# Scoring the last 64 keys of two quads of heads in one group of eight 32x64 tiles, with an issue order written out as a list

## The chip, the core and the metric

One core of a Trainium2 chip runs the whole program. The metric is device time in microseconds (us), the median of several executions. An operation runs on one of four computing engines: TensorE (PE in the profile, its weight loads PEld), VectorE (DVE), ScalarE (ACT) and GpSimd (POOL). SyncE (SP) issues most DMA transfers. Each engine works through its own instructions strictly in the order in which they were issued, and waits at an instruction whose inputs are not there.

## The reference

Four batches of 12 heads, 448 positions, head size 64; then a two-layer perceptron over 1792 tokens of 768 numbers with 2048 hidden units, all in float32.

```python
scores = scale * np.matmul(q, k.transpose(0, 1, 3, 2))
scores = cap * np.tanh(scores / cap)
scores = scores - np.max(scores, axis=-1, keepdims=True)
attn = np.exp(scores)
attn = attn / (np.sum(attn, axis=-1, keepdims=True) + 1e-09)
attn_out = np.matmul(attn, v)
x = attn_out.transpose(0, 2, 1, 3).reshape(B * S, H * D)
h = x @ w_in
out = np.maximum(0.01 * h, h) @ w_out
```

## The kernel before

**Attention.** The 48 heads go in 12 quads of four heads, a quad being two pairs. The head size of 64 is cut in two halves of 32 (`x`), so that a head's keys and queries fill one strip of 32 partitions and the four heads of a quad lie in the four strips of TensorE's array. `scores` (L490 to L506) makes the scores in four groups of keys. Groups 0 to 2 have 128 keys each: four tiles of 32x128 of the array work at once, one for each head, and two passes (`x` 0 and 1) are added (L505). Group `MID` has the last 64 keys: four tiles of 32x64 (L502), each of which uses one half of the columns, so that half the array stands still. Every float32 matmul of the program becomes two in the trace, so one group of scores is 16 matmuls and 16 weight loads. The scores land in the PSUM tiles `sc`, one for each pair, of two banks. ScalarE then takes tanh out of PSUM (L560) and exp in place (L563) into a ring of SBUF tiles `pf` (`exps` in the trace; some more of them lie in `w` for the first half of the pairs). `values` (L550) multiplies them with the value rows in two tiles of 128x64, `middle` (L525) does that for the last 64 keys in four tiles of 64x64. In parallel VectorE or GpSimd add the exponentials up into `t` (L568, L569, L571); from the fourth quad on VectorE transposes and reduces this sum (L592, L593), a matmul with a folding matrix (L597) adds across partitions, and VectorE takes reciprocals (L602), spreads them (L618) and scales the product out of the PSUM tile `po` (L633). `po` has two banks for these pairs, so the product of pair i+2 waits for the scaling of pair i.

**Perceptron.** The first 256 tokens go through both layers in plain float32 (L749, shapes 128x256) while attention still runs, which also brings the weights in: each of the 34 weight blocks is loaded (L657), converted by ScalarE (L686, L692) and VectorE (L694, L697) and stored to scratch memory. The next 512 tokens go through in split form (a rounded part and a rest, three matmuls instead of one; L749, 128x512). The last 1024 tokens go through a seven-product scheme (L1002, L1172). Finished rows of the second layer are transposed into the staging ring `ot` (L793) and stored (L714).

**Order.** Every piece of work is described by `plan.add(rank, cost, fn, ...)`: the engines that it may run on with a cost on each, what it reads and writes. `Plan.issue` (L115) then issues the 2237 steps one by one, taking the one that its cost table says can start first, ties going to the lower rank; ranks come from the formulas plus the tables of offsets in `T`. The engine of a step that may run on several is chosen there too.

**Start.** `cap`, then the keys, then the values of the first quad are issued on the SP queue, the queries on ScalarE's; VectorE computes the scale factors, then turns queries and keys (L481, L483, L484), then the first group of scores starts.

Of the kernel before, what the change touches and what calls it, by code (L numbers as in the profile page):

```python
# [20 lines left out]
    pf=6,  # L21
# [4 lines left out]
    ot=2,  # L26
# [23 lines left out]
    jc=19,  # L50
    ps=245,
# [3 lines left out]
    role={'duo C': -747.31, 'duo U': -735.34, 'duo a': 179.43, 'duo b': 124.52, 'duo d': 590.63, 'duo g': -972.64, 'duo vh': 66.56, 'duo vl': -126.79, 'duo vs': -257.1, 'duo ws dma': -667.59, 'duo z': 232.65, 'last uh': 813.04, 'last ul': -850.97, 'last wq dma': -1627.0, 'pair first first': -711.17, 'pair first.0 zero': -379.79, 'pair first.1 zero': -662.52, 'pair kT': 46.8, 'pair kT first': -31.97, 'pair kT.0 zero': 524.69, 'pair kraw dma': -251.58, 'pair kraw dma first': 172.22, 'pair kraw.0 dma zero': 256.19, 'pair late': -153.04, 'pair pf': 1229.42, 'pair pf exp': -636.67, 'pair pf first': -424.63, 'pair pf first exp': -1045.36, 'pair pf zero exp': -677.25, 'pair pf.0 zero': 476.57, 'pair pf.1 zero': -402.02, 'pair pf.2 zero': -57.0, 'pair pf.3 zero': -163.21, 'pair pf.4 zero': -330.08, 'pair pf.5 zero': -652.4, 'pair pf.6 zero': 135.96, 'pair pf.7 zero': -352.12, 'pair po': 46.47, 'pair po first': 98.34, 'pair po.0 zero': -814.17, 'pair po.1 zero': -331.16, 'pair po.2 zero': 507.3, 'pair po.3 zero': 960.61, 'pair qT': 507.24, 'pair qT first': 646.87, 'pair qT.0 zero': -560.63, 'pair qraw dma': 975.57, 'pair qraw dma first': -463.96, 'pair qraw.0 zero': -220.82, 'pair rs': 101.18, 'pair rt': 291.72, 'pair rt first': -532.24, 'pair rt.0 zero': 685.14, 'pair rt.1 zero': 177.61, 'pair sc': -78.62, 'pair sc first': 29.1, 'pair sc.0 zero': 29.75, 'pair sc.1 zero': -75.32, 'pair sc.2 zero': -234.87, 'pair sc.3 zero': -16.59, 'pair sums': 335.88, 'pair sums first': -694.63, 'pair sums.0 zero': -27.21, 'pair sums.1 zero': 548.07, 'pair sums.2 zero': -823.01, 'pair sums.3 zero': 66.32, 'pair t': -6.69, 'pair t first': -125.0, 'pair t.0 zero': -64.91, 'pair t.1 zero': -171.68, 'pair tT': 87.9, 'pair tail': -78.4, 'pair tot': -77.55, 'pair vc dma': 327.77, 'pair vc dma first': -73.96, 'pair vc.0 dma zero': -782.5, 'pair vc.1 dma zero': 431.37, 'pair wait': -253.82, 'pair x': -397.07, 'pair x first': 799.88, 'pair x.0 zero': 561.7, 'pair x.1 zero': 1748.4, 'pair x.2 zero': 215.71, 'pair x.3 zero': 900.12, 'pair xh': 233.42, 'pair xh first': 393.76, 'pair xh.0 zero': 535.24, 'pair xh.1 zero': 153.8, 'pair xl': -827.07, 'pair xl first': -666.27, 'pair xl.0 zero': 38.95, 'pair xl.1 zero': 1133.45, 'run Bh': 396.97, 'run Bl': -350.58, 'run g': -708.72, 'run late': -69.63, 'run late_T': -85.85, 'run wait_T': -395.49, 'side T': 692.46, 'side sH': -962.56, 'side sL': 132.33, 'sum p dma': -375.81, 'sum pr dma': 163.76, 'sum pre': 201.62, 'tile p': -171.41, 'tile store dma': 143.89, 'tile y': 420.39, 'tile yz': 34.48, 'unit g': -165.47, 'unit gh': 572.6, 'unit gl': -1821.34, 'unit gr first': 303.24, 'unit m': -295.94, 'unit m first': -98.85, 'unit ot': 570.96, 'unit ot first': 459.51, 'unit raw first': -22.51, 'unit scratch dma first': -952.64, 'unit store dma': 697.81, 'unit store dma first': 8.06, 'unit whi': -26.24, 'unit wlo': -50.07, 'unit wr dma first': 296.0, 'unit ws dma': -139.31, 'unit ws first': -9.13, 'x cap dma': -1133.33, 'x fixed_vx': -703.14, 'x fold': 302.79, 'x inv': -323.73, 'x regs': -707.36},  # L55
    pair=[-751.47, -917.18, -160.61, 298.32, 45.73, -549.43, -291.06, 148.77, -108.48, -102.5, 15.65, 416.32, 208.41, 216.63, -339.77, -85.19, -629.45, 975.97, 348.69, 982.9, -64.89, 260.92, -1123.87, -876.4, 0.0, 0.0, 0.0, 0.0, 0.0, 0.0],
# [5 lines left out]
    sum=[-74.38, 94.11, -560.41, -1031.6, 404.68, 85.84, -89.45, -386.3, -39.95, -117.43, -150.24, 303.72, 184.5, 188.74, 749.08, -126.77, -158.74, -502.96, -81.48, -387.42, -616.58, 21.56, 173.92, 18.59],  # L62
    tile=[-209.93, -102.29, -202.36, -40.16, 33.34, -362.19, 26.13, 30.99, -31.31, -32.81, -33.42, -34.86, -439.45, -32.85, 84.22, -60.17, 123.96, 119.05, -402.42, -104.85, -700.26, -6.29, 386.27, 346.62, 581.06, 33.84, 551.59, 123.05],
    phases=[(1000000000.0, {'pe': 33.33, 'dve': 0.44, 'pool': 0.03})],
)


def hundredths(x):
    return round(100 * x)


class Plan:
# [6 lines left out]

    SWITCH = 9
    LAT = {"act": 13, "dve": 12, "pool": 10, "pe": 20}

    def __init__(self):
# [1280 lines left out]
```

## Time and profile before

| | us |
|---|---|
| median of 3 runs | 643.89 (643.75 to 644.42) |
| the profiled execution | 643.21 |
| its span, first to last instruction | 641.4 |
| TensorE busy | 626.4 |
| VectorE busy | 505.3 |
| ScalarE busy | 348.2 |
| GpSimd busy | 149.6 |

The page gives for each engine the time in which it had an instruction in work. Because matmuls overlap each other, a group of matmuls is better read from the chain of work, where each piece counts only the time until the next one took over.

### The profile page before, as it was taken

What the parts mean: (1) busy time and instruction counts of PE and PEld (TensorE: products, weight loads), DVE (VectorE), ACT (ScalarE), POOL (GpSimd) and SP (SyncE); (2) the same over time, 40 slices, a digit from 0 to 9 for tenths busy, and PEclk for the clock granted to TensorE, in tenths of its full rate; (3) what the DMA queues carried; (4) which work ended last, traced back from release to release, by engine and by line L of the source; (5) the groups of instructions that cost most, each with busy time, mean ns of one, the idle gap of its engine ahead of it and who ended that gap; (6) DMA issues with size and microseconds to landing.
All of it is one profiled execution on the core that took longest, in us unless ns stands there. A gap on an engine that the chain in (4) does not pass through costs nothing.

```text
span 641.4 us, 9583 instructions
## 1 busy us (share of the span) xinstructions
PE 626.4 (98%) x3364; PEld 455.4 (71%) x3364; DVE 505.3 (79%) x801; ACT 348.2 (54%) x532; POOL 149.6 (23%) x180
## 2 busy tenths in 40 slices
PE   7999999999999999999999999999999999999996
PEld 4333655565656658686846688888888789999996
DVE  3989899999999987667858896776878999956640
ACT  4998688886856755246436343322334535743311
POOL 1032202311010314765644130130122320002210
PEclk9999999999999999999999999999999999999999
DMA  7974469758849767677774244220112063323422
GB/s 258 366 243 134 160 217 285 235 200 281 250 135 315 254 167 241 201 225 213 200 214 128 66 114 106 66 74 26 61 63 65 26 198 98 99 86 109 135 51 54
DMA packets 106151, 102.95 MB, mean 160 GB/s; under 512 B 29552, under 2 KB 86896, under 8 KB 106096
## 3 DMA queue, kind: packets, MB, share of 16 engines
q1 hardware_dynamic: 105184, 101.02, 52.1%
q10 hardware_dynamic: 912, 1.25, 0.7%
q8 instruction: 28, 0.46, 0.3%
q14 instruction: 27, 0.22, 0.1%
HBM read 77.86 MB, written 24.38 MB: 159 GB/s over the span
## 4 chain that ended last, share of the span: by engine, by line
PE 91%; DVE 5%; DMA 2%; ACT 1%; issue 1%; SPq 0%; DVEq 0%
PE m L749 35%; PE sc L1002 10%; PE po L550 9%; PE sc L1172 8%; PE sc L505 8%; PE po L1172 5%; PE m L1172 5%; PE po L1002 4%; PE sc L502 3%; PE m L1002 2%; PE po L525 1%; DMA raws<-in_k_dram 1%; DVE w L284 1%; DMA cap_sb<-in_cap_dram 1%; PE po L597 1%
## 5 line engine op out<-in xcount | busy, mean ns | idle before, releaser
L749 PE MATMUL m<-bank,ws 128*128 128x256 f32 x384 | 91.8, 388 | 0.0
L749 PEld LDWEIGHTS m<-bank,ws 128*128 128x128 f32 x384 | 70.1, 190 | 25.7 <-issue 10.1
L560 ACT ACTIVATE exps<-sc 128x896 f32<-128x896 f32 (+1 forms) x72 | 58.6, 837 | 49.5 <-PE sc L505 25.5
L277 ACT CAST w<-ws 128x384 fp32r<-128x384 f32 (+3 forms) x83 | 51.3, 632 | 51.2 <-PE m L749 24.5
L505 PE MATMUL sc<-heads 32*128 32x448 f32 x576 | 65.7, 560 | 4.3 <-ACT exps L560 2.0
L284 DVE TENSOR_TENSOR w<-ws,w 128x384 fp32r<-128x384 f32 (+3 forms) x84 | 63.5, 769 | 7.4 <-ACT w L277 5.9
L749 PE MATMUL m<-bank,w 128*128 128x512 f32 x288 | 68.8, 394 | 0.0
L749 PEld LDWEIGHTS m<-bank,w 128*128 128x128 f32 x288 | 53.2, 188 | 16.1 <-issue 4.8
L866 POOL TENSOR_TENSOR raws<-raws 128x128 f32<-128x128 f32 x96 | 55.2, 591 | 31.4 <-DMA raws<-scratch 28.3
L563 ACT ACTIVATE exps<-exps 128x896 f32<-128x896 f32 (+1 forms) x72 | 61.2, 872 | 0.7
L749 PE MATMUL m<-xh,w 128*128 128x512 f32 x192 | 61.2, 394 | 0.1
L505 PEld LDWEIGHTS sc<-heads 32*128 32x128 f32 x576 | 27.0, 184 | 33.8 <-issue 15.1
L550 PE MATMUL po<-exps,norm 128*64 128x448 f32 x232 | 48.8, 549 | 0.0
L749 PEld LDWEIGHTS m<-xh,w 128*128 128x128 f32 x192 | 36.0, 188 | 11.3 <-issue 2.7
L749 PE MATMUL m<-xl,w 128*128 128x512 f32 x96 | 37.4, 389 | 0.0
L284 POOL TENSOR_TENSOR w<-ws,w 128x384 fp32r<-128x384 f32 (+2 forms) x16 | 21.2, 1324 | 62.2 <-ACT w L277 53.7
L550 PEld LDWEIGHTS po<-exps,norm 128*64 128x64 f32 x232 | 14.7, 136 | 28.2 <-issue 21.1
L692 ACT ACTIVATE ws<-bank 128x768 f32<-128x768 f32 (+1 forms) x34 | 29.8, 881 | 8.7 <-PE m L749 8.5
L694 DVE SCALAR_TENSOR_TENSOR bank<-bank 128x768 int32<-128x768 int32 (+1 forms) x34 | 33.0, 977 | 1.8 <-ACT ws L692 1.6
L697 DVE SCALAR_TENSOR_TENSOR ws<-ws,bank 128x768 int32<-128x768 int32 (+1 forms) x34 | 30.5, 900 | 0.4
L686 ACT ACTIVATE bank<-bank 128x768 int32<-128x768 uint8 (+1 forms) x27 | 23.6, 876 | 3.5 <-DMA bank<-in_moe_w_out_dram 1.9
L571 POOL TENSOR_TENSOR norm<-norm,w 64x448 f32<-64x448 f32 x8 | 10.0, 1248 | 62.1 <-DVE norm L569 27.3
(220 smaller groups left out, 1230.8 us busy)
## 6 DMA issues: line engine op xcount, KB each, us to landing
ws<-scratch SPq DMA_DIRECT2D x38, 384.0 KB, 3.4
bank<-in_moe_w_in_dram SPq DMA_DIRECT2D x16, 768.0 KB, 7.4
scratch<-ws SPq DMA_DIRECT2D x22, 384.0 KB, 3.8
raws<-scratch SPq DMA_DIRECT2D x48, 128.0 KB, 3.3
sums<-raws SPq DMA_DIRECT2D x24, 256.0 KB, 3.0
raws<-in_k_dram SPq DMA_DIRECT2D x12, 448.0 KB, 5.6
raws<-in_q_dram SPq DMA_DIRECT2D x11, 448.0 KB, 4.6
norm<-in_v_dram SPq DMA_DIRECT2D x48, 96.0 KB, 3.3
```

What stands on the lines that cost most here:

```text
L277: nc.scalar.copy(o, i)
L284: ENG[eng].tensor_tensor(out=o, in0=a, in1=f32(b), op=ALU.subtract)
L505: nc.tensor.matmul(sc[r // 2][:, r % 2, 0:S], keys(a)[part4[r], x, P * g:P * g + P], queries(c)[part4[r], x], **flags)
L550: nc.tensor.matmul(at("po", 2 * i)[half[j], 0:S], at("vc", i)[:, j, g], pf(g)[:, j if wide(g) == 2 else 0], start=(g == 0), stop=(g == NG ...
L560: a = plan.add(r, {"act": ct}, lambda e, sc=sc, g=g: nc.scalar.activation(pf(g), sc(), AF.Tanh, scale=scale_of["tanh"]), vers("sc", [g]) + ...
L563: plan.add(r + 2, {"act": ct + 0.03}, lambda e, g=g: nc.scalar.activation(pf(g), pf(g), AF.Exp, scale=scale_of["exp"]), (), vers("pf", [g] ...
L694: a = plan.add(rank, {"dve": cv}, lambda e: nc.vector.scalar_tensor_tensor(out=word(1), in0=word(1), scalar=-0x80000000, in1=word(0), op0= ...
L697: plan.add(rank, {"dve": cv}, lambda e: nc.vector.scalar_tensor_tensor(out=z(), in0=z(), scalar=3, in1=word(1), op0=ALU.logical_shift_left ...
L749: nc.tensor.matmul(ps(), l, r, start=begins and some[0] == 0 and i == 0, stop=ends and some[-1] == len(cs) - 1 and i == len(ops) - 1)
L866: return plan.add(rank, cost, lambda e: ENG[e].tensor_tensor(out=o(), in0=a(), in1=b(), op=op), reads, writes, after=after, freed=freed, p ...
L1002: nc.tensor.matmul(ps(), l, r, start=start and x == 0, stop=x == len(ops) - 1, skip_group_check=not start)
L1172: nc.tensor.matmul(ps[t](), l, r, start=start and n0 == 0 and x == 0, stop=n0 == NK - 2 and x == len(ops) - 1, skip_group_check=not start)
```

## The change

- For the first four quads nothing changes in the scores. From the fifth on (`jm=4`) two neighbouring quads, (4,5), (6,7), (8,9) and (10,11), share one group `MID`: quad q's four tiles of 32x64 write bank 0 of the two `sc` tiles, quad q+1's four write bank 1, and `flipped` is turned round for the second quad, so that the eight tiles cover every strip and both column halves. The group is 32 matmuls and 32 weight loads. Its tanh and exp are then 128x896 for each `sc` tile, once for two quads. The second quad's keys and queries must be turned before the first quad's last group (`lead`, `jl=6`).
- The `pf` ring in SBUF grows from 6 to 7 tiles; two of them are kept for the joint group, five are left for the groups 0 to 2 (the tiles in `w` still come on top for the first half). `ot` shrinks from two tiles to one.
- For the first quad the keys are loaded in three transfers, the first 128 keys first and ahead of `cap`; the queries come in two halves; a tanh on one column is put behind them on ScalarE's queue; the turning is cut into four pieces, the first keys and the first half of the queries first, and the scale factors are computed after them.
- `issue` no longer plans: it goes through `STEPS`, a list of all 2237 steps. A number is a step's place in the order of the `plan.add` calls, the letter its engine (p TensorE, a ScalarE, v VectorE, g GpSimd, s SyncE). All offsets in `T` are zero and unused.

```diff
-    pf=6,
+    pf=7,
-    ot=2,
+    ot=1,
+    jm=4,
+    jl=6,
...
+STEPS = """
+    3s 6a 5s 7v 8v 9v 10v 11p 1g 4v 0g 665s 676s 15s 667a 666a 677v 68s 67s 687s 33s 71v 668v 669v 688v 69v 70v 654s 698s 2a 34a 16a 35a 17a 12p
...
-    def issue(self, phases):
+    def issue(self, order):
...
+        issued = set()
+        for item in order.split():
+            n, eng = int(item[:-1]), self.ENGINES[item[-1]]
+            s = steps[n]
...
+            assert deps <= issued and n not in issued and eng in s["cost"], n
+            issued.add(n)
             s["fn"](eng)
...
+    JM = T["jm"]
+    joint = lambda q_: 0 if q_ < JM else 1 + (q_ - JM) % 2
+    mid_of = lambda i: (4 * (i - 2) + 3, 1) if joint(i // 2) == 2 else (4 * i + 3, 0)
...
+            free_ = list(range(n_pf - 2)) + (list(range(n_pf, n_pf + n_more)) if wide_ else [])
+            for g in range(4):
+                for i in (2 * q_, 2 * q_ + 1):
+                    if g == 3:
+                        out[4 * i + g] = -1 if joint(q_) == 2 else n_pf - 2 + i % 2
+                    else:
+                        out[4 * i + g] = free_[turn_ % len(free_)]
+                        turn_ += 1
...
+    def first_loads(n):
+        t, src = raw4("kraw"), rows_of(k)
+        by_tile = lambda a: a[:, 0:4 * MID].rearrange("p (r g) d -> p r g d", g=MID)
+        if n == 0:
+            nc.sync.dma_start(out=by_tile(t)[:, :, 0], in_=by_tile(src)[:, :, 0])
+            nc.sync.dma_start(out=cap_sb, in_=cap.to_broadcast([P, 1]))
+            return
+        nc.sync.dma_start(out=by_tile(t)[:, :, 1:], in_=by_tile(src)[:, :, 1:])
+        nc.sync.dma_start(out=t[:, 4 * MID:], in_=src[:, 4 * MID:])
+
+    def first_queries():
+        t, src = raw4("qraw"), rows_of(q)
+        for h in range(2):
+            nc.scalar.dma_start(out=t[:, HB * h:HB * h + HB], in_=src[:, HB * h:HB * h + HB])
+        nc.scalar.activation(warm, zeros, AF.Tanh)
...
-    flipped = lambda i: i % 2
+    flipped = lambda i: i % 2 ^ (joint(i // 2) == 2)
...
+            for x in range(2):
+                flags = dict(start=x == 0, stop=x == 1)
+                for r in range(4):
+                    if g < MID:
+                        nc.tensor.matmul(sc[r // 2][:, r % 2, 0:S], at("kT", q_)[part4[r], x, P * g:P * g + P], at("qT", q_)[part4[r], x], **flags)
+                        continue
+                    for c in range(2 if joint(q_) else 1):
+                        c_ = half[r % 2 ^ flipped(i0 + 2 * c + r // 2)]
+                        nc.tensor.matmul(sc[r // 2][c_, c, 0:S], at("kT", q_ + c)[part4[r], x, far:S], at("qT", q_ + c)[part4[r], x], **flags)
...
-        plan.issue(T["phases"])
+        plan.issue(STEPS)
```

## Rows read from the trace of the kernel before

**Rows 1.** Page: busy time, granted clock in 40 slices, chain by engine.

```profile
PE 626.4 (98%) x3364; PEld 455.4 (71%) x3364; DVE 505.3 (79%) x801; ACT 348.2 (54%) x532; POOL 149.6 (23%) x180
...
PEclk9999999999999999999999999999999999999999
...
PE 91%; DVE 5%; DMA 2%; ACT 1%; issue 1%; SPq 0%; DVEq 0%
```

**Rows 2.** Busy time of each engine by stage, us from the span's start.

```profile
core 0: us, PE busy (x) PEld busy (x) DVE busy (x) ACT busy (x) POOL busy (x), PEclk, DMA share, GB/s
0.00:36.00 36.00, 30.90 (x182) 13.82 (x184) 24.69 (x46) 27.16 (x36) 5.11 (x17) 1.00 0.93 315
36.00:66.00 30.00, 29.17 (x199) 11.08 (x193) 26.71 (x52) 25.32 (x37) 9.00 (x9) 1.00 0.54 170
...
101.00:231.00 130.00, 130.00 (x776) 76.09 (x775) 123.37 (x194) 98.14 (x133) 19.84 (x14) 1.00 0.75 238
231.00:400.00 169.00, 168.85 (x831) 121.27 (x831) 126.47 (x180) 77.92 (x117) 73.27 (x109) 1.00 0.62 173
...
510.00:642.00 132.00, 122.50 (x694) 120.09 (x692) 87.89 (x141) 51.46 (x96) 14.87 (x9) 0.99 0.35 101
```

**Rows 3.** Chain of work in order of time: start us, us, what.

```profile
75.42 5.38 PE m L749 x24
80.80 1.72 PE sc L505 x16
82.52 2.41 PE po L550 x12
84.92 0.91 PE po L525 x8
...
96.26 1.66 PE sc L502 x16
...
355.03 1.66 PE sc L502 x16
```

**Rows 4.** Weight loads of L502: durations ns min/median/max, and eight at 176.87 us.

```profile
L502 PEld LDWEIGHTS sc<-heads x192: 127/131/132, 18.7 to 355.8; 32*64 32x64 f32 x192
...
176.87 0.21 PEld L502 LDWEIGHTS sc<-heads 32*64 32x64 f32 x8 [0.33 <-issue]
```

**Rows 5.** ScalarE's tanh, shapes apart: busy us, mean ns, idle before.

```profile
L560 ACT ACTIVATE exps<-sc 128x896 f32<-128x896 f32 x56 | 50.5, 919 | 36.6 <-PE sc L505 25.5 <-PE po L550 8.0 <-PE po L525 2.4
...
L560 ACT ACTIVATE exps<-sc 128x448 f32<-128x448 f32 x16 | 8.1, 547 | 12.8 <-PE sc L502 12.8
```

**Rows 6.** Timeline of the start: start us, us, engine, line, operation.

```profile
4.29 0.59 SPq L657 DMA_DIRECT2D bank<-in_moe_w_in_dram  x1
...
6.06 1.15 DVE L481 STREAM_TRANSPOSE heads<-raws 128x448 f32<-128x448 f32 x2
...
8.01 1.81 PE L505 MATMUL sc<-heads 32*128 32x448 f32 x16 [0.47 <-DVE heads L483]
...
9.88 1.73 ACT L560 ACTIVATE exps<-sc 128x896 f32<-128x896 f32 x2 [1.78 <-PE sc L505]
9.99 0.56 DVE L688 TENSOR_SCALAR bank<-bank 128x768 int32<-128x768 int32 x1 [1.20 <-DMA bank<-in_moe_w_in_dram]
```

**Rows 7.** Adding up exponentials on VectorE and GpSimd: busy us, mean ns, idle before.

```profile
L568 DVE TENSOR_TENSOR norm<-exps 128x896 f32<-128x896 f32 x15 | 16.3, 1085 | 2.9 <-PE m L554 2.5 <-ACT exps L563 0.4
...
L568 POOL TENSOR_TENSOR norm<-exps 128x896 f32<-128x896 f32 x5 | 11.0, 2204 | 46.6 <-DVE norm L592 46.6
```

**Rows 8.** The staging tile: two transposes, the store between them, and all its landings.

```profile
383.67 0.70 DVE L793 STREAM_TRANSPOSE ot<-m 128x512 f32<-128x512 f32 x1
...
384.40 3.78 SPq L714 DMA_DIRECT2D out_dram<-ot  x8
...
389.56 0.72 DVE L793 STREAM_TRANSPOSE ot<-m 128x512 f32<-128x512 f32 x1 [1.07 <-PE m L749]
...
DMA to landing us min/median/max: 1.5/1.7/6.5
```

More of the change, by code (lines that the diff above doesn't have):

```diff
@@ L131, in issue @@
                 deps.update(writers.get(old, ()))
[L132 to L172 removed]
+            assert deps <= issued and n not in issued and eng in s["cost"], n
+            issued.add(n)
+            s["fn"](eng)
+        assert len(issued) == len(steps)
 @with_exitstack
@@ L290, in softcap_attention_mlp @@
     zeros = const.tile([P, 1], F32, name="zeros")
+    warm = keep.tile([P, 1], F32, name="warm")
     ones = const.tile([P, 64], F32, name="ones")
@@ L323, in softcap_attention_mlp @@
         plan.ring(tag, 1)
-    alias("sc", [tile_of(f"sc_{j}", [P, 2, 512], F32, psum) for j in range(2)], [i % 2 for i in range(n_pairs) for _ in range(4)])
+    alias("sc", [tile_of(f"sc_{j}", [P, 2, 512], F32, psum) for j in range(2)], [-1 if g == 3 and joint(i // 2) == 2 else i % 2 for i in range(n_pairs) for g in range(4)])
     two_banks = [tile_of(f"po_{j}", [P, 512], F32, psum) for j in range(2)]
@@ L492, in scores @@
             sc = [at("sc", NG * (i0 + j) + g) for j in range(2)]
-            keys = (lambda w: split_of("k", w)) if parted else (lambda w: at("kT", q_))
-            queries = (lambda w: split_of("q", w)) if parted else (lambda w: at("qT", q_))
-            terms = (("h", "h"), ("h", "l"), ("l", "h")) if parted else (("h", "h"),)
-            ops = [(x, a, c) for x in range(2) for a, c in terms]
-            for n, (x, a, c) in enumerate(ops):
-                flags = dict(start=n == 0, stop=n == len(ops) - 1)
-                if g == MID:
-                    for r in range(4):
-                        c_ = half[r % 2 ^ flipped(i0 + r // 2)]
-                        nc.tensor.matmul(sc[r // 2][c_, 0, 0:S], keys(a)[part4[r], x, far:S], queries(c)[part4[r], x], **flags)
-                else:
-                    for r in range(4):
-                        nc.tensor.matmul(sc[r // 2][:, r % 2, 0:S], keys(a)[part4[r], x, P * g:P * g + P], queries(c)[part4[r], x], **flags)
@@ L516, in plan_quad @@
+        for g in range(NG if joint(q_) < 2 else MID):
+            both = (q_, q_ + 1) if g == MID and joint(q_) else (q_,)
+            plan.add(r0 + T["pq"] + 5 * g, {"pe": 2 * BOTH}, lambda e, g=g: scores(g), [(t, q) for q in both for t in ("kT", "qT")],
+                     [("sc", NG * (i0 + j) + g) for j in range(2)], mode=1 if g < MID else 3)
         plan_pair(i0)
@@ L542, in plan_pair @@
         late = late_of(i)
-        wide = lambda g: 2 if g < MID else 1
+        wide = lambda g: 2 if g < MID or joint(i // 2) else 1
         pf = lambda g: at("pf", NG * i + g)[:, 0:wide(g)]
@@ L554, in total @@
                 nc.tensor.matmul(at("po", 2 * i + 1)[half[j], 0:S], ones, tt()[:, j], start=True, stop=True)
-        for g in range(NG):
+        for g in range(NG if joint(i // 2) < 2 else MID):
             sc = lambda g=g: at("sc", NG * i + g)[:, 0:wide(g), 0:S]
@@ L929, in softcap_attention_mlp @@
     d_banks = [("m", 0), ("m", 1)]
-    before = {("sc", j): [("sc", NG * (n_pairs - 2 + j % 2) + MID)] for j in range(4)}
+    before = {("sc", j): [("sc", NG * (n_pairs - 2 + j % 2) + MID - 1)] for j in range(4)}
     before.update({("po", j): [("po", 2 * i) for i in (n_pairs - 2, n_pairs - 1)] + [("tot", i) for i in (n_pairs - 2, n_pairs - 1)] for j in range(2)})
```

213 lines of the change are left out of this document (140 added, 73 removed).

## Prediction

> **What bounds the kernel now.** I read the page first: TensorE is busy 98% of the span, holds 91% of the chain that ended last, and has the full clock in every slice [rows 1]. So the change has to be priced in TensorE's time. Second, the stages [rows 2], for where TensorE is not busy: the first 36 us (5.1 us idle), 36 to 66 us (0.8), and the end (132.0 - 122.5 = 9.5 us, of which 0.6 lie beyond the span). Between 101 and 400 us, where the joint groups will lie, it idles 0.15 us in 299. There no wait is left to be won; only less matmul time helps there, and any new wait is lost. The same rows show who would be next: from 101 to 231 us VectorE is busy 123.4 of 130 us, ScalarE only 98.1, GpSimd 19.8. Third, the chain in order of time [rows 3], for what a group really occupies: a group of four tiles of 32x64 (L502) takes 1.66 us, as long as a full group of 128 keys (L505, 1.72 us) that does twice the work. Of the twelve L502 pieces the eight from 96.26 to 355.03 us are those of quads 4 to 11, which the change merges.
>
> **The joint groups.** Removed: eight L502 groups, 8 x 1.66 = 13.28 us. Added: four groups of eight tiles. An L502 group is 16 matmuls in four waves of four, 1.66 / 4 = 0.415 us a wave. If eight tiles run as well together as four, the new group is again four waves and takes 1.66 us: 13.28 - 4 x 1.66 = 6.64 us saved. If they do not overlap at all, it takes 3.32 us and nothing is saved. Three near rows speak for the first end [rows 3]. L550 runs two tiles that share all rows and differ in columns: 12 matmuls in 2.41 us, 0.40 us for each two. L525 runs four tiles of 64x64, two in each row strip: 8 matmuls in 0.91 us. L505 writes four whole banks at once, as much PSUM as the eight half-height tiles will. What no row shows is 32 loads and 32 matmuls in that time. Eight loads of 131 ns each begin and end within 0.21 us [rows 4], so one follows the next after (210 - 131) / 7 = 11 ns; 16 instructions of a wave need about 0.18 us by that, under the wave's 0.415. They are hidden, except that the first wave starts later; I take 1.75 us for a joint group: 4 x (3.32 - 1.75) = 6.3 us saved. By L525's 0.91 us for two waves it would be 1.82, which costs another 0.3 us.
>
> A rule of the Trainium skill speaks against this group: "TensorEngine Tiling (Array Packing)", section "Gotcha 1: PSUM Pressure", says that different row tiles cannot access the same PSUM bank simultaneously. In the joint group each bank is written by two row strips, in opposite halves. But L502 does that already (strips 0 and 1 write one bank) and still needs 1.66 us, no more than L505, whose four tiles have a bank each [rows 3]; taking turns it would need about twice that. By the row the rule doesn't hold for opposite halves, and the sum stays at 6.3 us; by the rule it would be 0.
>
> ScalarE: for two quads four tanh of 0.547 us become two of 0.919 [rows 5], and exp alike: some 0.7 us less for each joint group. ScalarE isn't the bound from 66 us on, so this is worth 0. The second quad's keys and queries are turned earlier: the same VectorE instructions, and the list has those of quad 5 ahead of quad 4's first group. 0, covered by the TensorE work listed between the last of them and the joint group: `middle`, two groups of scores and five weight blocks, which at 0.91, 1.72 and 5.38 / 2 us [rows 3] are 18 us.
>
> **The start.** Now the first matmul of scores begins at 8.01 and the first tanh at 9.88 us; the first weight block is issued at 4.29 and is there at 9.99 [rows 6]. From its first tanh on ScalarE has hardly a gap: 27.2 us busy in the first 36 [rows 2], so what counts is when ScalarE begins. In the list it has the two conversions of weight block 1 ahead of its first tanh. These wait for a load that stands behind four transfers on SP's queue instead of six, so it is issued 2 x 0.59 = 1.2 us sooner [rows 6]. If it also lands 1.2 us sooner, ScalarE begins at about 8.8 instead of 9.9 us. The first scores themselves need less turning (an estimate by width from 1.15 us for two of 448 columns: 1.2 us instead of the 1.95 from 6.06 to 8.01). Bounds: 2.0 us gained if ScalarE then never waits, 2.0 us lost if the weights land no sooner, for then the first tanh stands behind two conversions, each about as long as its own 0.92 us [rows 5], from 9.99 us on. I take 1.0 us gained, as the issue row is the nearest.
>
> **The order.** Little of it can be priced by one row, so I read the list for three things.
> - *VectorE to GpSimd.* The first sum of exponentials goes to GpSimd for 13 of 24 pairs (now 5), at 2.20 instead of 1.09 us [rows 7]. This takes 8 x 1.09 = 8.7 us off VectorE, most of it where VectorE is 95% busy, but makes the path to the scaling 1.1 us longer each time. Between the product of pair i and that of pair i+2, which waits for the scaling, the list has at least 12.1 us of TensorE work (pairs 10 to 12: two groups of scores, `values`, `middle`, two weight blocks, by [rows 3]), far more than the 1.1 us. Covered, unless the path has no slack at all now.
> - *The shorter ring.* From pair 12 on five `pf` tiles serve the groups 0 to 2 of a quad, six of them; the sixth tanh reuses the first tile, so it waits for `values` of the first pair. From the third group's end to the next group the chain is tanh 0.92, exp (about the same), `values` 2.41, tanh 0.92 [rows 3, 5], 5.2 us and somewhat more with hand-overs. For quad 6 the list has one weight block (2.69 us) before `values` and one after, for quad 8 3.1 and 1.3 us of them, for the others more. Covered, with under 1 us to spare: 0 to 2 us lost.
> - *One staging tile.* A transpose into `ot` must now wait until the last store has landed: 3.78 us of issue plus 1.7 us (up to 6.5), 5.5 us at least, against 389.56 - 383.67 = 5.9 us between two transposes now [rows 8]. At the end of the second layer's split part the list puts that store behind two other loads, and behind the transpose on VectorE stand the weights of the first products of the next stage. 0 to 3 us.
>
> Together 0 to 5 us lost; I take 1.0, near the lower end, as each has cover in the list. The stages after 400 us keep their work; 0, with 1.5 us to either side for other waits at 510 us and later.
>
> **Sum.** Against the profiled execution, 643.2 us (span 641.4 and 1.8 around it): 643.2 - 6.3 - 1.0 + 1.0 = 636.9. The median of the runs is 0.7 us above that execution, so 637.6; I say 637.5.
>
> **Rivals.**
> - *Eight tiles do not run at once* (two strips on one bank, or loads that wait for a multiply of the same strip). The joint group then takes 3.3 us, the 6.3 us are gone: about 643.9. Against it stand L502, L550 and L525. 8%.
> - *The cover is too thin.* Ring and staging tile cost 3 to 5 us instead of 1: about 641, still faster. 10%.
> - *The vector chain becomes the bound*: slower. Place: the 18 pairs from the fourth quad on, whose sums go to GpSimd in 11 cases. Price: 11 x 1.12 = 12.3 us if all of it reaches TensorE by way of the scaling and the `po` banks, for VectorE, in strict order, then stands at an instruction that waits for GpSimd while the next quad's turning is queued behind it. It decides once 7.3 us (the gains) get through, some 0.7 us for each of the 11. All of it: 649; I put it at 647. For it: VectorE has only 6.6 us to spare in 130. Against it: the work moved off VectorE there, and GpSimd 85% idle. 13%.
>
> **Chances.** Forecast 69%; its own range is 633.8 (all gains at their bounds, 643.9 - 6.64 - 2.0 - 1.5) to 640.6 (3 us lost on top). With 10, 8 and 13% beyond, the range takes in the case of no gain, 643.9 with 1 us to either side for start and order: 633.8 to 645.0. A measurement of this kernel tells about 0.2%, 1.3 us, from no change. Faster: 69 + 10 = 79%; within 0.2%: 8%; slower: 13%.
>
> **What would show it.** Four pieces of the joint line of 1.7 to 1.8 us in the chain instead of eight of 1.66; if they take 3.3, the first rival. TensorE's idle time from 66 to 400 us at most 2 us; if it is 5 or more, the rows of who it waited for name the ring (tanh before scores), the vector chain (GpSimd or VectorE before `values`) or the staging tile (at about 390 us). The first tanh's and first conversion's time give the start. The forecast is wrong if the order costs more than 5 us in places that the old trace can't show.

## The result: slower by 0.8%, where 1% faster was forecast

| | before | after |
|---|---|---|
| median of the runs, us | 644.0 (643.75 to 644.42) | 649.26 (647.84 to 650.24) |
| ratio | 1 | 1.0079, 95% interval 1.0063 to 1.0096 |
| span of the profiled execution, us | 641.4 | 648.5 |
| granted clock, mean of the span | 0.998 | 0.989 |

The forecast was 637.5 us with a range up to 645.0; both the sign and the range were wrong. (A slip of the front part: the planner of before issues 2257 steps; 2237 are those of the new list.)

The page of after, busy time, granted clock and the chain by engine, answers to [rows 1]:

```profile
PE 621.1 (96%) x3364; PEld 452.9 (70%) x3364; DVE 514.6 (79%) x847; ACT 325.9 (50%) x487; POOL 185.7 (29%) x168
...
PEclk8799999999999999999999999999999999999998
...
PE 64%; DVE 4%; ACT 3%; DMA 2%; issue 1%; POOL 1%; ACTq 0%; SPq 0%; DVEq 0%; POOLq 0%
```

TensorE is 5.3 us less busy than before, although the span is 7.1 us longer. So the work was saved, and idle time took more than its place. The granted clock, full in every slice before, is below it in the first two, and in the last, behind the last multiply. The chain's 64% is not to be compared with the 91% of before: this chain could be followed back only to 152.7 us, while its shares are of the whole span.

Busy time by stage, after, answers to [rows 2]:

```profile
core 0: us, PE busy (x) PEld busy (x) DVE busy (x) ACT busy (x) POOL busy (x), PEclk, DMA share, GB/s
0.00:36.00 36.00, 27.59 (x156) 12.56 (x160) 19.54 (x40) 22.85 (x30) 6.84 (x18) 0.86 0.75 238
...
66.00:101.00 35.00, 34.65 (x199) 22.30 (x196) 33.43 (x53) 27.59 (x40) 10.17 (x7) 1.00 0.82 256
101.00:231.00 130.00, 129.13 (x811) 78.42 (x810) 121.16 (x183) 98.98 (x129) 42.67 (x26) 1.00 0.79 242
231.00:396.00 165.00, 165.00 (x829) 119.16 (x828) 135.58 (x232) 72.77 (x103) 62.07 (x68) 1.00 0.65 173
396.00:520.00 124.00, 117.91 (x508) 94.00 (x507) 84.95 (x147) 36.01 (x73) 31.64 (x29) 1.00 0.21 62
```

From 66 to 396 us, where the joint groups lie, TensorE idles 0.35 + 0.87 + 0 = 1.2 us, before 0.15: the middle is nearly as full as it was. From 396 to 520 us, a stage that the change was not about, it idles 6.1 us.

**The ledger.** I cut both executions at four events that both have: the first group of scores of the fourth quad, the first multiply of the first two-group products (L1002 before, L1118 after), the first of the second ones (L1172, L1288) and the end of the last multiply. All figures in us; the runs below are cut the same way.

| kernel | to the fourth quad | to the first products | first products | second products | tail | span |
|---|---|---|---|---|---|---|
| before | 55.0 | 345.2 | 115.6 | 119.5 | 6.0 | 641.4 |
| after | 57.1 | 338.9 | 123.7 | 119.6 | 9.2 | 648.5 |
| difference | +2.1 | -6.4 | +8.1 | +0.1 | +3.2 | +7.1 |

The four joint groups are in the second column, and all of their gain is there. It is given back in the first products, in the tail and at the start.

The joint group itself, in the chain of after (start us, us, what), answers to the L502 pieces of [rows 3]:

```profile
205.27 1.72 PE sc L621 x16
206.99 3.22 PE m L865 x14
210.21 2.41 PE po L666 x12
212.62 1.49 PE m L865 x6
214.11 0.14 PE po L713 x2
214.24 1.69 PE sc L625 x32
```

32 matmuls take 1.69 us, where sixteen took 1.66 before; all four joint groups take as long. The 32 begin in four waves of eight, the eight of a wave within 0.05 us, the waves 0.38 to 0.43 us apart, as the sixteen before did in four waves of four. 4 x (3.32 - 1.69) = 6.5 us saved.

**The start**, timeline of after (start us, us, engine, line, operation, idle before and who ended it), answers to [rows 6]:

```profile
2.82 1.02 SPq L773 DMA_DIRECT2D bank<-in_moe_w_in_dram  x2
...
6.88 1.79 PE L621 MATMUL sc<-heads 32*128 32x448 f32 x16
...
10.03 0.89 ACT L808 ACTIVATE ws<-bank 128x768 f32<-128x768 f32 x1 [6.85 <-DMA bank<-in_moe_w_in_dram]
10.82 0.86 ACT L802 ACTIVATE bank<-bank 128x768 int32<-128x768 uint8 x1
11.59 1.71 ACT L676 ACTIVATE exps<-sc 128x896 f32<-128x896 f32 x2
...
13.35 3.37 PE L621 MATMUL sc<-heads 32*128 32x448 f32 x16 [4.69 <-ACT exps L676]
...
18.56 3.37 PE L621 MATMUL sc<-heads 32*128 32x448 f32 x16 [1.84 <-ACT exps L676]
```

The scores come 1.1 us sooner, and their tanh 1.7 us later, for ScalarE has two conversions ahead of it. Their load was issued 1.47 us sooner than before and is there at 10.03 us instead of 9.99. TensorE, idle for 4.69 us, then needs 3.37 us for a group that takes 1.79 us elsewhere. The windows give the granted clock (the number before the last two of a row):

```profile
9.00:13.30 4.30, 0.00 (x0) 0.00 (x0) 0.56 (x1) 3.27 (x5) 0.00 (x0) 0.93 1.08 358
13.30:16.80 3.50, 3.37 (x16) 1.22 (x16) 2.44 (x3) 1.69 (x3) 0.00 (x0) 0.50 1.06 341
16.80:18.50 1.70, 0.00 (x0) 0.00 (x0) 0.90 (x2) 1.70 (x3) 0.00 (x0) 0.50 1.01 329
18.50:22.00 3.50, 3.44 (x18) 1.36 (x20) 1.29 (x4) 1.72 (x4) 1.73 (x1) 0.50 0.89 291
```

0.50 is the lower of the two levels, 1.2 of 2.4 GHz, and two groups fall into it.

The +2.1 us of the first column are those of one execution. The start of after's list stands unchanged in e_four, e_split, e_tail, e_eng, e_late, e_duo and e_duo2 below, and the eight profiled executions reach the fourth quad at 54.5 to 57.4 us. The granted clock was 0.50 for about 10 us in the four that took 56.4 to 57.4 us, for about 7 us in the three that took 55.8 to 56.4, and for about 3 us in the one that took 54.5.

**The first products.** Who TensorE waited for from 395.93 to 519.63 us, after (engine, line, releaser: us in total, times, longest):

```profile
PE sc L1118 <- ACT bank L337: 2.5, 4, 0.9
PE sc L1118 <- DVE bank L1128: 1.2, 2, 0.9
PE sc L1118 <- DVE xh L1128: 0.9, 1, 0.9
PE sc L1118 <- ACT xh L337: 0.7, 1, 0.7
PE sc L1118 <- ACT wait L337: 0.7, 1, 0.7
PE sc L1118 <- POOL w L344: 0.2, 1, 0.2
```

Ten short waits, 6.2 us together, nine of them for results being taken out of the PSUM banks `sc` (evictions). Before, there was one in this stage:

```profile
PE sc L1002 <- DVE xh L1012: 0.9, 1, 0.9
```

The stage as a whole, before and then after:

```profile
400.23:515.87 115.64, 114.76 (x505) 94.44 (x504) 88.85 (x144) 42.18 (x81) 26.73 (x23) 1.00 0.18 54
395.93:519.63 123.70, 117.61 (x505) 93.71 (x504) 84.65 (x146) 36.08 (x73) 31.34 (x29) 1.00 0.21 61
```

The other 2.9 of the 8.1 us are time in which TensorE is recorded as busy, 117.6 us instead of 114.8 with the same 505 matmul records. They go with the ten waits too: multiplies begin 0.23 us apart and last 0.39, so the last one before a wait counts with all its length, and the group right behind a wait is longer (nine in 2.33 instead of 2.20 us).

**The tail.** SP's queue, after:

```profile
603.44 0.34 SPq L1231 DMA_DIRECT2D ws<-scratch  x1
618.80 0.78 SPq L1323 DMA_DIRECT2D out_dram<-norm  x2
619.67 0.38 SPq L1231 DMA_DIRECT2D ws<-scratch  x1
620.10 15.41 SPq L1323 DMA_DIRECT2D out_dram<-norm  x26
635.70 8.26 SPq L1323 DMA_DIRECT2D out_dram<-bank  x8
```

SP issues nothing from 603.8 to 618.8 us, because the next step of its list is the store of a tile that isn't done before; 26 transfers and the last eight stores follow with hardly a gap. Before, SP had issued all but the last eight by 624.3 us:

```profile
599.75 24.57 SPq L1207 DMA_DIRECT2D out_dram<-norm  x20
628.64 8.06 SPq L1207 DMA_DIRECT2D out_dram<-bank  x8
```

### The profile page after: what moved, and what is told of

Its sections match the earlier page's. It is cut to its first block, busy times and chain, and to the rows that moved or that the text cites. A ratio compares the mean times of both kernels' runs of the same rounds, so it can differ in the third digit from the quotient of the medians.

```text
span 648.5 us, 9565 instructions
## 1 busy us (share of the span) xinstructions
PE 621.1 (96%) x3364; PEld 452.9 (70%) x3364; DVE 514.6 (79%) x847; ACT 325.9 (50%) x487; POOL 185.7 (29%) x168
## 4 chain that ended last, share of the span: by engine, by line
PE 64%; DVE 4%; ACT 3%; DMA 2%; issue 1%; POOL 1%; ACTq 0%; SPq 0%; DVEq 0%; POOLq 0%
PE m L865 25%; PE sc L1118 10%; PE sc L1288 7%; PE po L1288 4%; PE po L666 4%; PE m L1288 4%; PE sc L621 3%; PE po L1118 3%; PE m L1118 2%; DMA scratch<-ws 1%; DVE w L344 1%; PE po L641 1%; ACT bank L337 1%; PE sc L625 1%; DMA out_dram<-bank 0%
## 5 line engine op out<-in xcount | busy, mean ns | idle before, releaser
L865 PE MATMUL m<-bank,ws 128*128 128x256 f32 x384 | 89.4, 386 | 1.2 <-DVE ws L813 0.6
L676 ACT ACTIVATE exps<-sc 128x896 f32<-128x896 f32 x68 | 59.8, 897 | 42.1 <-PE sc L621 28.2
L337 ACT CAST w<-ws 128x384 fp32r<-128x384 f32 (+3 forms) x77 | 47.6, 644 | 51.3 <-PE m L865 16.4
L344 DVE TENSOR_TENSOR w<-ws,w 128x384 fp32r<-128x384 f32 (+3 forms) x73 | 56.3, 782 | 9.7 <-ACT w L337 9.1
L344 POOL TENSOR_TENSOR w<-ws,w 128x384 fp32r<-128x384 f32 (+2 forms) x27 | 35.7, 1332 | 80.1 <-ACT w L337 40.0
L684 POOL TENSOR_TENSOR norm<-exps 128x896 f32<-128x896 f32 x11 | 23.4, 2123 | 67.1 <-DVE norm L708 26.6
L687 POOL TENSOR_TENSOR norm<-norm,exps 64x448 f32<-64x448 f32 x17 | 24.3, 1427 | 63.1 <-ACT exps L679 32.8
L810 DVE SCALAR_TENSOR_TENSOR bank<-bank 128x768 int32<-128x768 int32 (+1 forms) x34 | 35.1, 1036 | 3.1 <-ACT ws L808 2.9
L813 DVE SCALAR_TENSOR_TENSOR ws<-ws,bank 128x768 int32<-128x768 int32 (+1 forms) x34 | 33.9, 997 | 1.7
L982 POOL TENSOR_TENSOR raws<-raws 128x128 f32<-128x128 f32 x41 | 22.3, 556 | 39.1 <-DVE raws L982 19.3
```

What stands on the lines that cost most here:

```text
L337: nc.scalar.copy(o, i)
L344: ENG[eng].tensor_tensor(out=o, in0=a, in1=f32(b), op=ALU.subtract)
L676: a = plan.add(r, {"act": ct}, lambda e, sc=sc, g=g: nc.scalar.activation(pf(g), sc(), AF.Tanh, scale=scale_of["tanh"]), vers("sc", [g]) + ...
L810: a = plan.add(rank, {"dve": cv}, lambda e: nc.vector.scalar_tensor_tensor(out=word(1), in0=word(1), scalar=-0x80000000, in1=word(0), op0= ...
L813: plan.add(rank, {"dve": cv}, lambda e: nc.vector.scalar_tensor_tensor(out=z(), in0=z(), scalar=3, in1=word(1), op0=ALU.logical_shift_left ...
L865: nc.tensor.matmul(ps(), l, r, start=begins and some[0] == 0 and i == 0, stop=ends and some[-1] == len(cs) - 1 and i == len(ops) - 1)
```

## The experiments

The same ledger for the runs whose list is a variant of that of after; the last column is the median of the runs, in us.

| kernel | to the fourth quad | to the first products | first products | second products | tail | median |
|---|---|---|---|---|---|---|
| after | 57.1 | 338.9 | 123.7 | 119.6 | 9.2 | 649.3 |
| e_four | 56.9 | 338.3 | 123.6 | 119.6 | 9.2 | 649.2 |
| e_split | 54.5 | 346.0 | 123.7 | 119.6 | 8.9 | 655.1 |
| e_start | 53.8 | 339.4 | 123.7 | 119.6 | 8.7 | 647.1 |
| e_warm | 54.1 | 338.1 | 123.7 | 119.6 | 8.8 | 646.7 |
| e_tail | 56.4 | 338.1 | 123.7 | 118.3 | 6.4 | 645.7 |
| e_eng | 57.4 | 338.1 | 121.5 | 119.6 | 8.9 | 647.3 |
| e_late | 56.4 | 354.0 | 117.3 | 119.5 | 5.8 | 655.1 |
| e_duo | 55.8 | 353.0 | 122.9 | 118.0 | 9.2 | 660.3 |
| e_duo2 | 56.4 | 338.2 | 116.6 | 119.5 | 6.8 | 639.1 |
| e_best | 52.6 | 338.1 | 116.6 | 119.6 | 7.0 | 635.8 |

**Eight tiles at once, or four and four?**

```diff
 # group MID alone, its loops in short
-            for x in range(2):
-                for r in range(4):
-                    for c in range(2 if joint(q_) else 1):
+            for c in range(2 if joint(q_) else 1):
+                for x in range(2):
+                    for r in range(4):
```

> Against the changed kernel (649.3 us): only the order inside the joint step differs, the four tiles of the first quad (16 matmuls) before the four of the second, no longer eight at once. Theory A, that eight tiles at once are what saves time: the four joint steps take 2 x 1.66 = 3.32 us instead of 1.69, so 4 x 1.63 = 6.5 us more, about 655.8 us. Rival B, that the eight-fold overlap is worth nothing because the end of the attention part is set by another engine: within 1 us of 649.3. In either case the stages after 400 us are as long as in the changed kernel.

Measured: 649.16 us (648.88 to 649.93). Theory A's 655.8 is refuted, but not for the reason of B. In the chain of this run the 32 matmuls still take 1.83 us in the first joint step and 1.72 in the other three, as here:

```profile
152.89 1.72 PE sc L619 x32
```

The second quad's sixteen run beside the first quad's although they stand behind them in the queue: the 32 begin in four waves, each of four multiplies and, 0.05 us later, four more. So "eight at once" in the source isn't what saves time; that the two groups stand next to each other may be. The next run tests that.

```diff
 # order of e_four, between the two quads of a joint step
+                    if c:
+                        nc.tensor.matmul(sc[0][:, 0, S + 16:S + 32], fold, ones[:, 0:16], start=True, stop=True)
```

> Against the run with the two quads' tiles one after the other (649.2 us), in which 32 matmuls still took 1.72 us: the same order, but between the two quads' sixteen matmuls stands one small multiply over all rows and columns (128x128 by 16 columns, into a corner of the scores' bank that nobody reads). It costs some 0.3 us itself, by the 0.34 us of the two-instruction multiply of the row sums. Theory A, that the two quads' tiles run side by side whenever nothing of another shape stands between them, and that this is the whole gain: each joint step takes 2 x 1.66 + 0.3 = 3.6 us, 4 x 1.9 = 7.7 us more, 656 to 657.5 us. Rival B, that the gain lies elsewhere (one change of tile shape fewer, or 32 loads queued together): 1.72 + 0.3 + at most 0.2 us for each, about 650.5 to 651.5 us.

Measured: 655.06 us (654.38 to 656.46). The chain of this run at the second joint step:

```profile
152.22 0.14 PE po L714 x2
152.36 1.66 PE sc L621 x16
154.02 0.33 PE sc L617 x2
154.34 1.66 PE sc L621 x16
156.01 6.03 PE m L866 x27
```

1.66 + 0.33 + 1.66 us: with one multiply over the whole array between them the two groups run one after the other. Theory A holds for the joint step; the time stays a little under its range. The second column of the ledger is 7.7 us longer than in e_four, 4 x 1.93, as worked out; that the medians differ by only 5.9 is the start, at least in the profiled execution: there the clock was back at 1.00 by 16.8 us (first column 2.4 us shorter). The Trainium skill, "TensorEngine Tiling (Array Packing)", section "Tiling Modes", "Key Properties", says that tiles work independently of each other and that a change of the tiling drains TensorE. The trace agrees with the first: 1.69 us together. With the second it is compatible, 3.65 us with the multiply between; but that multiply also needs every row and column, so this run can't tell a drain at a change of shape from a wait for the whole array.

**The start.** In the list the two conversions (667a 666a), the VectorE steps that use them (668v 669v) and two loads into their buffer (654s 698s) go behind the second group's exponentials (19a):

```diff
-665s 676s 15s 667a 666a 677v 68s ...  668v 669v ... 654s 698s 2a 34a 16a 35a 17a 12p 36a 18a 13p 37a 19a
+665s 676s 15s 677v 68s ... 2a 34a 16a 35a 17a 12p 36a 18a 13p 37a 19a 667a 666a 668v 669v 654s 698s
```

> Against the changed kernel (649.3 us): the two ScalarE conversions of weight block 1 and the two VectorE steps that use them, with the two loads that reuse their buffer, stand behind the second group's exponentials in the list, nothing else moves. Theory A, that the start lost its time because ScalarE stood at a conversion whose load landed at 10.03 us, which let TensorE idle 4.69 us and its granted clock fall to 0.5: the first tanh begins at about 8.9 instead of 11.59 us (2.7 us), groups 0.1 and 0.2 take 1.8 us instead of 3.37 (up to 3.2 us more), and the conversions' 1.75 us come back later, since ScalarE is the bound there: 3 to 4 us gained, 645.3 to 646.3 us, with the clock at 1.00 from 13 to 23 us. Rival B, that this stretch is bound by ScalarE's sum of work and the conversions are only moved: 648.5 to 649.3 us.

Measured: 647.09 us (646.06 to 647.57), 2.2 us less than after, short of A and beyond B. The tanh began at 9.56, not 8.9 us: ScalarE now waited for the scale factor, which the list computes on VectorE behind the second half of the turning. And the clock still fell, after idle stretches of 2.60 and 1.85 us, to 0.50 from 16.8 to 18.5 us. A's place is right, since the first column is 3.3 us shorter; its clock was wrong.

The next run fills the idle stretch of TensorE instead (cut from the kernel):

```diff
             scores of group 0.0
+            for _ in range(18 if q_ == 0 and g == 0 else 0):
+                nc.tensor.matmul(tiles["m"][0][:, 0:S], still[:, 0:P], still, start=True, stop=True)
```

> Against the changed kernel (649.3 us): behind the first group of scores TensorE gets 18 multiplies of zeros into a bank that nobody reads before it is written again; they lie in its idle 4.69 us, and the load that ScalarE waits for stays as it is. It prices the fall of the clock by itself. Theory A, the granted clock fell because TensorE stood idle: it stays at 1.00, groups 0.1 and 0.2 take 1.8 instead of 3.37 us, ScalarE's two waits of 1.8 us for scores shrink to about 0.3 us, and 2 to 3.2 us are gained: 646.1 to 647.3 us. Rival B, the clock falls whatever TensorE does there: 649.3 us or a little more, clock 0.50 from 13 to 23 us. Rival C, the clock stays high but the time is bound by ScalarE's work and comes back before 57 us: clock 1.00 and 649 us.

Measured: 646.66 us (644.94 to 648.31), A. Nothing but idle time of TensorE was filled, by multiplies that compute nothing. The windows of this run:

```profile
9.00:13.30 4.30, 3.92 (x20) 3.24 (x18) 0.56 (x1) 3.31 (x5) 0.00 (x0) 1.00 1.09 363
13.30:16.80 3.50, 1.78 (x16) 0.72 (x16) 2.44 (x3) 3.27 (x5) 0.00 (x0) 1.00 1.06 338
```

The conversions stand where they were, the first tanh begins at 11.60 as in after, and the clock stays at 1.00; the group takes 1.78 us. So the fall of the clock alone cost about 2.6 us (649.3 - 646.7, between medians of runs that reach from 647.84 to 650.24 and from 644.94 to 648.31). Without it the new start was 0.9 us shorter than the old one, in spite of the late tanh (54.1 against 55.0, one execution of each). The Trainium skill, "TensorE: Matmul & The Clock Gate", section "Why this matters for your kernels", asks that TensorE be kept from idle gaps between bursts for this reason. For this gap the trace agrees: 0.50 after it, 1.00 when it was filled; the falls in e_start and e_best came after shorter ones.

**The tail.** One store (2170s) goes behind those of the fifth product (2106s, 2108s, 2110s); only SP's entries are shown:

```diff
-2170s 2207s 2108s 2044s 2106s 2164s 2110s
+2207s 2108s 2044s 2106s 2164s 2110s 2170s
```

> Against the changed kernel (649.3 us): in SP's queue the store of one tile of the sixth product (ready at 618.8 us) stands behind those of the fifth product instead of ahead of them, nothing else moves. Theory A, that this one store kept SP from 603.8 to 618.8 us with finished tiles and the last product's weight loads behind it, so that SP's stores ended late: the 3.3 us that the tail grew by are gone, 645.5 to 646.5 us, and the time from the last matmul to the end is again 6 to 6.5 us instead of 9.3. Rival B, the tail is set by the eight last stores and their issue time alone: 649 us, with 9 us after the last matmul.

Measured: 645.74 us (643.85 to 646.76), the tail 6.4 instead of 9.2 us. A. SP's queue in this run:

```profile
601.88 0.82 SPq L1228 DMA_DIRECT2D ws<-scratch  x2
605.19 26.33 SPq L1320 DMA_DIRECT2D out_dram<-norm  x28
631.62 6.65 SPq L1320 DMA_DIRECT2D out_dram<-bank  x8
```

It starts on the same stores 15 us sooner. The second products are another 1.3 us shorter, likely because the last loads of their weights stood behind the same store: two waits of TensorE for subtractions on GpSimd, 0.4 and 0.3 us, are gone.

**The first products.** Two runs put the steps of the last stages back into the order of before, placed among the others by how far TensorE had come. In e_duo these were the sums of blocks and the first products, in e_late also the second products and their stores.

> Against the changed kernel (649.3 us): the steps of the block and first two-group products (those that run from 400 to 520 us) are issued in the order and on the engines of the kernel before, all others as in the changed list. Theory A, that the list's order and choice of engines in this stage lost 8.1 us: the stage takes 115 to 117 us instead of 123.7 and TensorE idles there 1 to 2 us instead of 6.1: 641 to 643 us. Rival B, that the buffers that were changed (one staging tile instead of two, seven exponential tiles) or another state at the stage's entry cost it: 647 to 649 us, with the same waits as before the edit.

> Against the changed kernel (649.3 us): all steps behind the second layer's split part (blocks, first and second two-group products, stores) in the order and on the engines of the kernel before, the attention part as in the changed list. Theory A, that nothing but order is lost after 400 us: 8.1 us in the stage from 400 to 520 us and 3.3 us in the tail come back, 637 to 639 us, which is the forecast but for the start. Rival B, that the last stage only inherits a worse position and gives no more than the first stage alone: 641 to 643 us. Rival C, that buffers rather than order cost the time: 647 to 649 us.

Measured: 660.28 us (659.76 to 663.55) and 655.11 us (653.9 to 655.75). Both misses: slower, and by a loss that none of the theories had. The second column is 14 to 15 us longer. In e_late TensorE waited there as follows, from 385 to 412 us, with a mean granted clock of 0.75:

```profile
PE m L862 <- DVE ot L906: 4.9, 1, 4.9
PE m L862 <- DVE w L338: 4.1, 1, 4.1
```

The two orders had been cut together badly: on VectorE the transpose that frees a bank of TensorE stood behind preparations of the next products, which wait for a load, and on SP the stores of the output tiles stood behind loads of those products. That is a fault of these kernels and tells nothing of the change. What does tell something is the stage itself, once begun: 117.3 us in e_late, with three waits of 2.2 us together. In e_duo it took 122.9 us, against theory A; there the ten waits had also become three, but one of them, 4.8 us, lies at the stage's end, where the old order meets the new one again and VectorE has preparations of the second products ahead of an eviction. So this seam between the two orders was mended: the sums of blocks stay in the new list, and the last three output tiles are transposed and stored earlier among the next products' steps.

```diff
 # e_late, sums of blocks as in the list of after, and
+1242v 1243s (output tile 61: transpose, store) ahead of 1545s, a load for the second pair of products
+1262v 1263s (tile 64) behind 1515v;  1282v, 1283s (tile 67) behind the loads of the third pair
```

> Against the changed kernel (649.3 us): the first two-group products, the second ones and the stores in the order and on the engines of the kernel before, but the blocks' sums in the changed list, and the last three output tiles' transposes and stores arranged so that each store stands ahead of the loads of the next products (in the earlier runs a store stood behind such a load and VectorE waited some 15 us for the single staging tile before 408 us). Theory A, that order and choice of engines in this stage lost the 8 us and the tail 3.3: the stage from the first to the second two-group products takes 116 to 118 us instead of 123.7, the tail 6 us, 638 to 641 us. Rival B, that the single staging tile makes the old order impossible, so that the list had to give up time there: TensorE waits 5 us or more before the stage for a transpose into that tile, 645 us or more.

(The reason given there for the earlier loss, a wait for the single staging tile, was wrong: the rows above name VectorE's queue.)

Measured: 639.06 us (638.67 to 639.72), ratio to before 0.9916 (0.9892 to 0.9940). A, though the tail took 6.8 us. Busy time in its first products, and the waits of TensorE there:

```profile
394.62:511.20 116.58, 114.82 (x505) 94.44 (x504) 90.67 (x149) 43.03 (x82) 25.98 (x22) 1.00 0.21 60
```

```profile
PE sc L1115 <- DVE xh L1125: 0.9, 1, 0.9
PE sc L1115 <- DVE bank L1125: 0.9, 1, 0.9
```

With the same steps, buffers and joint groups the stage takes 116.6 instead of 123.7 us, two waits instead of ten, and GpSimd has 22 steps instead of 29. One staging tile does not stand in the way. With the order of the last stages undone the change is 0.8% faster than before instead of 0.8% slower.

Is it the choice of engines or the sequence?

```diff
 # first products only: the list's sequence, 67 letters changed to the engine of before, e.g.
-1518g   (a subtraction on GpSimd)
+1518v
```

> Against the changed kernel (649.3 us): the order of the list stays, but in the first two-group products 67 steps run on the engine that the kernel before gave them (fewer on GpSimd, more on ScalarE). Theory A, that the choice of engines lost the time (a subtraction takes 1.02 us on GpSimd and 0.55 on VectorE): the stage from 396 to 520 us shrinks by 4 us or more, 645 us or less, and TensorE's waits there fall from 6 to under 3 us. Rival B, that it is the sequence on each engine: within 2 us of 649.3 or slower, since the sequence was made for other engines.

Measured: 647.28 us (645.78 to 647.72), 2.0 us less, the stage 121.5 us. It is at B's edge: TensorE's waits there fall only from 6.2 to 4.7 us, so the engines explain about 2 of the 7 us, the sequence (or both together) the rest. The trace of after speaks for the sequence too: in five of its ten waits the engine that evicts had stood idle for 3 to 8 us and began when TensorE's group just before had ended. Which of the steps in the sequence cost it stays open.

**The joint groups under the old planner**, the list left out altogether:

```diff
-        plan.issue(STEPS)
+        plan.issue(T["phases"])     # with the planner and the offsets of the kernel before
```

> Against the kernel before (644.0 us): the joint groups, the new start and the new numbers of buffers, but the order is made by the planner of the kernel before, with its parameters, and not by the list. Theory A, that joint groups are worth 6.3 us under any good order and the list is what lost time: 636 to 640 us. Rival B, that the planner's parameters were fitted to the old steps and give a worse order for the new ones, so that the list was needed: 644 to 655 us. The duration of a joint group, 1.69 us, is the same in both.

> Against the kernel before (644.0 us): as the run under the old planner, but without joint groups (each quad scores its last 64 keys by itself); the new start, seven exponential tiles and one staging tile stay. It prices these without the list. Theory A: they cost or give at most 2 us under the planner, 642 to 646 us, and the run with joint groups is 5 to 7 us faster than this one. Rival B: one staging tile instead of two costs the stages after 380 us 3 us or more: 647 us or more, with waits for a store ahead of the transposes into it.

Measured: 696.54 us (691.6 to 700.47) with joint groups and 698.88 us (696.93 to 701.01) without. Both above every forecast. The old offsets belong to the old steps; with another start and other rings the planner makes an order that waits in many places (TensorE 12.9 us for tanh ahead of scores in e_plan, in eight of them). That the offsets are the reason is likely, but no run fitted new ones. A joint group takes 1.69 us there too:

```profile
114.80 1.69 PE sc L572 x32
```

but the medians of the two runs lie only 2.3 us apart, and their runs overlap. So what the joint groups are worth in an order that leaves TensorE waiting isn't shown: neither 0 nor 6.5 us is excluded, and the planner made a different order for each. The run without joint groups, meant to price ring and staging tile, priced the mismatch and says nothing on them.

**All remedies together:** e_duo2, with the conversions moved as in e_start, the scale factors (4v 2a) ahead of the second half of the turning, and seven multiplies of zeros behind the first scores.

> Against the run with the old order of the two-group products (639.1 us): the start is mended too. The two conversions of weight block 1 stand behind the second group's exponentials, the scale of the tanh is worked out ahead of the second half of the turning, and seven multiplies of zeros lie behind the first group of scores. Theory A, that the late load and the fall of the clock are separate losses (2.2 and 2.6 us when each was taken away by itself) that overlap in part: the first tanh at about 8.9 us, no stretch with a granted clock under 1.00 before 30 us, 3 to 4.5 us gained, 634.6 to 636.1 us, under both kernels. Rival B, that ScalarE's sum of work bounds the first 57 us, so that the second remedy adds nothing to the first: 636.5 to 637.5 us.

Measured: 635.79 us (635.31 to 637.22), ratio to before 0.9878 (0.9861 to 0.9895): 1.2% faster than before and, by the medians, 2.1% faster than after. That is A in time, 3.3 us less than e_duo2. The first tanh begins at 8.18 us and the first column is 52.6 us, 3.8 less than in e_duo2. The expectation for the clock failed again: it was 0.72 from 13.3 to 16.8 us and 0.56 from 16.8 to 18.5, after a later idle stretch of 1.84 us.

## Why the prediction was wrong, step by step

- **What bounds the kernel.** Right: TensorE, nowhere idle in the middle. That was also the reason why any new wait would be lost, and it held in the stage in which I expected none.
- **The joint groups, -6.3 us.** Right in size: 1.69 us each instead of 1.75, 6.5 us. That two strips write opposite halves of one bank together is confirmed. The mechanism was put too narrowly: the eight tiles need not be issued together (e_four), as long as no multiply over the whole array separates the two groups (e_split).
- **The start, -1.0 us.** Wrong in sign: +2.1 in the profiled execution (the eight that share this start took 54.5 to 57.4 us, against 55.0 before). Of the two ends named, the bad one came true: the load lands no sooner (10.03 against 9.99) although it is issued 1.47 us sooner, and the first tanh stands behind two conversions. I had taken the gain because the issue row was "nearest". The step that failed is "If it also lands 1.2 us sooner": the row of the landing, 9.99 us, was as near and was the one that counts. A second term was missing, the granted clock. With the conversions ahead of the tanh TensorE has 4.69 us of nothing to do; that cost about 2.6 us (e_warm) and was not in the bounds as such.
- **The order in the middle, +1.0 us.** Right, at its lower end. The second column fell by 6.4 us, and the joint groups give 6.5. From 66 to 396 us TensorE waits three times, 1.2 us together, each time for VectorE at a perceptron multiply; neither a tanh ahead of scores (the shorter ring), nor a `po` bank, nor the staging tile is among them.
- **The stages after 400 us, 0 with 1.5 to either side.** This is the step that failed: "keep their work; 0". They keep their work, but not their order, and the measured terms are +8.1 and +3.2 us. I read the list for three things, all of them ahead of 400 us, and priced the rest by the number of its steps. A list that replaces a planner replaces it in every stage; 67 steps of the first products had changed their engine and one store had moved ahead of five others, both readable in the list beforehand. That these are order and choice of engines alone, and not the buffers, is shown by e_tail (-3.5 us) and e_duo2 (-10.2 us for the last stages together). Which steps of the first products' sequence cost most of the 8.1 us stays open.
- **The rivals.** Eight tiles not at once: refuted (1.69). Cover too thin: not seen. The vector chain as the bound: not in the middle, where I put it; the waits in the first products are of its kind (TensorE behind evictions on ScalarE and VectorE), but in another stage and by another cause. The slower outcome had 13%, all of it for the wrong mechanism; that its price, 647 to 649 us, lies near the 649.3 measured is a coincidence.

The sum with the measured terms: 643.2 - 6.4 + 2.1 + 8.1 + 0.1 + 3.2 = 650.3 for the profiled execution, which took 650.24.

## What to carry to other kernels

When an order is replaced, price it in every stage that it orders: compare for each engine which steps moved past which, above all stores and loads on a queue that stops at the first one that isn't ready, and steps that changed to a slower engine. A gain on the bounding engine counts only if the order gives it no new waits elsewhere: the joint groups saved 6.5 us in after as in e_duo2, and the one kernel was slower than before, the other faster. And small tiles shared TensorE here when their groups stood next to each other; look for a multiply over the whole array between them before looking at the loop order.

## What the runs showed of the hardware

- Groups of small tiles overlap across instructions issued one after the other: 16 and 16 matmuls of 32x64 tiles in opposite column halves take 1.72 us, and 3.65 us with a two-instruction full-array multiply (0.33 us) between.
- The granted clock fell to 0.50 after 4.69 us without a matmul, and 18 multiplies of zeros in that gap kept it at 1.00. It also fell for a short time when the gaps were only 2.60 and 1.85 us (e_start), or 0.22 and 1.84 us (e_best), while a gap of 1.84 us in the kernel before left it at 1.00. What separates these cases isn't settled by these runs.
- A load issued 1.47 us sooner among the first transfers landed at the same time, 10.03 against 9.99 us. From 2.8 to 10 us the 16 DMA engines were busy for 0.95 of the time and moved 292 GB/s, before 0.93 and 304. The second weight block, issued 0.5 us behind the first (before: 4.7 us), could be used at 12.35 us, before at 16.05. That the engines were the limit and shared between the two is likely, but no run took a transfer away to show it.
